# Routed attention and a spectral gate on one core: pairwise start, PV in pairs, a re-buffered last batch

## The chip, the core and the metric

The kernel runs on one core of a Trainium2 chip. The metric is the time of one execution in device microseconds; "span" is the part of it that the profile covers, from the first instruction to the last (the time reads some 1.7 us above the span). The engines are PE (matmul), DVE (vector), ACT (scalar), POOL (general) and SP (issues most transfers). The program gives each engine its own list of instructions and makes it wait for others by semaphores.

## The reference, cut to what matters

```python
# q, k, v: (4, 8, 768, 64), centroids: (8, 16, 64), float32
q_assign = argmax(einsum(q / |q|, c / |c|))        # a cluster for each query
k_assign = argmax(einsum(k / |k|, c / |c|))        # and for each key
scores = where(q_assign == k_assign, q @ k.T / 8, -1e9)
attn = softmax(scores) @ v                         # (4, 8, 768, 64)
x = attn, heads side by side                       # (4, 768, 512)
x1, x2, x3 = split(x @ w_proj)                     # w_proj: (512, 1536)
conv = irfft(rfft(x2) * rfft(filter_fft))          # along the 768 positions
out = (x1 * conv * x3) @ w_out
```

## The kernel before

Heads come in eight groups of four (two groups make a batch), each in two pairs. A head pair goes through six key tiles of 128 keys. The Python code does not fix the order of instructions: it describes operations with an estimated length, a due time and the buffers they read and write, and a list scheduler (`place`) puts them in order on each engine.

```python
NPB = 6        # P tiles (one head's exp of one key tile), 6 in turn
...
# in place(): which of the operations that could start goes next on an engine
t0 = min(c[0] for c in cand)
c = min((c for c in cand if c[0] <= t0 + wait * (c[1].kind == "urgent") + 1e-9),
        key=lambda c: (c[1].due, c[1].seq))
...
# in attention(): one key tile sk of a head pair
for hp in range(2):
    def sc(e, hp=hp, sk=sk, h=h):              # scores: two matmuls of 384 columns
        ...
    op(("PE", .34), sc, ..., kind="score")
    ex = op(("ACT", .82 + ...), ...activation(T.p[s]..., Act.Exp, scale=0.125), ...)
def pv(e, sk=sk):                              # P times V: eight matmuls 128x64 by 385
    ...
op(("PE", 1.37), pv, due, ..., kind="pv")
if sk:                                         # sums of P for the denominator, per head
    for hp in range(2):
        def acc(e, hp=hp, sk=sk):
            x = T.p[slots[hp, 0]][:, :S] if sk == 1 else T.acc[hp]
            T.nc.vector.tensor_tensor(T.acc[hp], x, T.p[slots[hp, sk]][:, :S], op=Alu.add)
        op(("DVE", .95), acc, ...)
...
# in hyena(): column tile dt of a batch; yy and od have one buffer, x3 two
op(("POOL", 1.9), lambda e, dt=dt, xb=xb: T.nc.gpsimd.tensor_tensor(
    T.y2[:, dt], T.yy[:]..., T.x3[xb][:]..., op=Alu.mult), ...)
...
# the start
for z in range(4): load_qk(0, z // 2, z % 2, z * .1)
load_v(0, 2.0); routing(0)                     # all four heads at once, then 8 mask rows
for z in range(4): load_qk(1, z // 2, z % 2, 9 + z)
tables()                                       # loads of the filter, its spectrum
```

"Masks" are rows that say which cluster a query or key belongs to; they are moved into the operands of the score matmuls by transfers of 24 KB. "Routing" makes them. `tables` makes the spectrum of the filter, `hyena` is all that follows attention in a batch.

The softmax here doesn't subtract the row's maximum and nothing guards it: scores larger than these inputs give would overflow.

## Time and profile before

| | before |
|---|---|
| time, median of 3 (range) | 468.88 us (466.34 to 470.32) |
| span of the profiled run | 467.4 us |
| first exp / first PV | 34.8 / 54.7 us |
| first PV to end of last PV | 351.8 us |
| end of last PV to end | 60.9 us |
| mode changes of PE (into and out of PV, routing and denominator products) | 236 |

The profile counts an instruction's whole duration as busy time, also where POOL or DVE holds it up: an addition of 3245 ns, shown below, is in the 121.6 us of its group (64 of 1899 ns) in full. Two groups of the page matter later; after the bar stand busy us, mean ns of one, then the engine's idle time before them and what ended it:

```profile
L503 DVE TENSOR_TENSOR acc<-acc,p 128x768 f32<-128x768 f32 x128 | 127.5, 1034 | 9.5 <-ACT p L482 9.3
L667 POOL TENSOR_TENSOR y<-yy,x 128x768 bf16<-128x768 f32 x16 | 32.3, 2020 | 108.4 <-DVE yy L663 89.0
```

The additions on DVE that follow the first of a head take 1034 ns in the mean, and POOL's products 2020 where ten of the 16 take 1799 to 1832. By start and end in the trace, 132 of all 160 additions have no work of POOL beside them, and none of these takes over 960 ns. The twelve of over 1 us lie beside POOL's other large group (L622, sums of the spectrum: eight), its products (two) or its casts (two), which will matter.

### The profile page before, as it was taken

The numbers are of one execution on the slowest core, as the hardware profiler recorded it, in microseconds if no ns is written. First come the engines' busy times: TensorE is split into PE (matmuls) and PEld (weight loads), VectorE is DVE, ScalarE is ACT, GpSimd is POOL, SyncE is SP. The second block draws the span as 40 slices with busy tenths as digits, with TensorE's granted clock in tenths as the row PEclk, the third lists the DMA queues.
The fourth block names the chain that finished last, engine by engine and source line by source line (L and its number), as shares of the span: only waits on it lengthen the run. The fifth ranks groups of instructions, "written<-read, shape, count | busy, mean of one in ns | idle before, by whom it ended". The sixth has DMA issues, their size and how long they took to land. (4 is left out here: it accounts for less than half of the span.)

```text
span 467.4 us, 6821 instructions
## 1 busy us (share of the span) xinstructions
PE 417.5 (89%) x2431; PEld 180.4 (39%) x2444; DVE 361.4 (77%) x557; ACT 274.3 (59%) x418; POOL 93.0 (20%) x94
## 2 busy tenths in 40 slices
PE   4745799999999998999999899999997999889846
PEld 3422333443434444434443344434333443334412
DVE  7885767899899898896759997978769788825550
ACT  5663276877775578477954687476654456424213
POOL 4420000000100813011005322030105312202540
PEclk9895899999999999999999999999999899979977
DMA  8999500522631234115610232123110010111003
GB/s 195 231 202 238 115 14 1 138 70 53 155 84 49 72 70 102 32 36 179 183 35 19 67 70 67 41 81 127 45 37 17 1 35 3 35 79 57 1 0 135
DMA packets 67226, 37.06 MB, mean 79 GB/s; under 512 B 56636, under 2 KB 62328, under 8 KB 67192
## 3 DMA queue, kind: packets, MB, share of 16 engines
q1 hardware_dynamic: 65992, 34.50, 28.5%
q0 software_dynamic: 1056, 2.10, 2.5%
q8 instruction: 19, 0.31, 0.3%
q14 instruction: 15, 0.12, 0.1%
q10 hardware_dynamic: 144, 0.03, 0.0%
HBM read 30.66 MB, written 6.48 MB: 79 GB/s over the span
## 5 line engine op out<-in xcount | busy, mean ns | idle before, releaser
L482 ACT ACTIVATE p<-pair 128x768 f32<-128x768 f32 x192 | 149.2, 811 | 58.8 <-PE pair L478 39.9
L493 PE MATMUL pair<-p,vraw 128*64 128x385 f32 x768 | 147.6, 507 | 1.0 <-DVE hm L350 0.4
L503 DVE TENSOR_TENSOR acc<-acc,p 128x768 f32<-128x768 f32 x128 | 127.5, 1034 | 9.5 <-ACT p L482 9.3
L478 PE MATMUL pair<-aug,aug 128*128 128x384 bf16 (+1 forms) x384 | 86.3, 331 | 9.8 <-ACT p L482 4.8
L493 PEld LDWEIGHTS pair<-p,vraw 128*64 128x64 f32 x768 | 48.1, 139 | 66.6 <-issue 61.8
L622 POOL TENSOR_TENSOR y<-tm 128x512 bf16<-128x512 f32 x24 | 38.3, 1604 | 114.6 <-DVE tm L618 90.7
L478 PEld LDWEIGHTS <-aug 128*128 128x128 bf16 (+1 forms) x384 | 33.6, 98 | 54.6 <-issue 39.8
L667 POOL TENSOR_TENSOR y<-yy,x 128x768 bf16<-128x768 f32 x16 | 32.3, 2020 | 108.4 <-DVE yy L663 89.0
L634 PE MATMUL bank<-xT,wpj 128*128 128x384 bf16 x256 | 48.7, 327 | 2.8 <-DVE x L641 1.3
L387 PE MATMUL bank<-ident,qkraw 128*128 128x128 f32 x192 | 34.3, 305 | 11.9 <-DMA qkraw<-in_q_dram 10.7
L503 DVE TENSOR_TENSOR acc<-p,p 128x768 f32<-128x768 f32 x32 | 29.6, 955 | 19.3 <-ACT p L482 9.1
L220 POOL CAST aug<-qkT 64x768 bf16<-64x768 f32 x11 | 11.2, 1018 | 138.9 <-ACT qkT L218 69.7
L387 PEld LDWEIGHTS bank<-ident,qkraw 128*128 128x128 f32 x192 | 24.1, 154 | 29.5 <-issue 11.9
L618 DVE TENSOR_TENSOR tm<-bank,hm 128x512 f32<-128x512 f32 x48 | 30.5, 680 | 6.0 <-PE bank L365 4.7
L634 PEld LDWEIGHTS <-wpj 128*128 128x128 bf16 x256 | 23.6, 97 | 27.7 <-issue 13.8
L679 PE MATMUL bank<-wout,y 128*128 128x512 bf16 x91 | 26.8, 436 | 7.2 <-POOL y L667 6.0
L218 ACT COPY qkT<-bank 128x384 f32<-128x384 f32 x43 | 20.2, 479 | 16.4 <-PE bank L387 16.2
L218 ACT COPY x<-bank 128x384 f32<-128x384 f32 x23 | 11.0, 478 | 23.8 <-PE bank L634 19.3
L218 ACT CAST aug<-qkT 64x768 bf16<-64x768 f32 x28 | 23.2, 830 | 0.7
L218 ACT COPY ob<-bank 128x512 f32<-128x512 f32 x22 | 12.7, 584 | 18.0 <-PE bank L679 16.4
L605 PE MATMUL bank<-wpj,uT 128*128 128x512 bf16 x92 | 22.4, 380 | 0.7 <-DVE uv L220 0.5
L663 DVE TENSOR_TENSOR yy<-bank,od 128x384 f32<-128x384 f32 x32 | 16.3, 550 | 8.0 <-ACT od L218 5.9
(114 smaller groups left out, 397.9 us busy)
## 6 DMA issues: line engine op xcount, KB each, us to landing
qkraw<-in_q_dram SPq DMA_DIRECT2D x32, 192.0 KB
qkraw<-in_k_dram SPq DMA_DIRECT2D x32, 192.0 KB
vraw<-in_v_dram SPq DMA_DIRECT2D x8, 768.0 KB
rb<-dr SPq DMA_DIRECT2D x30, 192.0 KB
out_dram<-ob SPq DMA_DIRECT2D x11, 512.0 KB
y<-in_moe_filter_fft_dram SPq DMA_DIRECT2D x4, 384.0 KB
wpj<-in_moe_w_proj_dram POOLq DMA_DIRECT2D x1, 1536.0 KB, 12.2
aug<-ohT SPq DMA_DIRECT2D x64, 24.0 KB
```

The source lines that it names most:

```text
L218: T.nc.scalar.copy(out, in_)
L387: T.nc.tensor.transpose(ap(h)[:, ts(t, 128)], T.qkraw[s][:, 3 * ch + t].rearrange("p h d -> p (h d)"), T.ident)
L478: T.nc.tensor.matmul(two(h)[:, ch, :384], ag[1][:K, ts(sk, 128)], ag[0][:K, ts(ch, 384)], start=True, stop=True)
L482: ex = op(("ACT", .82 + (1.28 if first[0] is None else 0)), lambda e, h=h, s=s: T.nc.scalar.activation(T.p[s][:, :S].rearrange("p (a b) -> ...
L493: T.nc.tensor.matmul(o[64 * hp:64 * hp + 64, ch, :385], T.vraw[aset][:, 2 * pr + hp, sk * D:(sk + 1) * D], T.p[slots[hp, sk]][:, 384 * ch: ...
L503: T.nc.vector.tensor_tensor(T.acc[hp], x, T.p[slots[hp, sk]][:, :S], op=Alu.add)
L605: T.nc.tensor.matmul(ap(h), f[:, e_, kt, ts(m, 128)], T.wpj[:, kt, DM:2 * DM], start=(kt == 0), stop=(kt == ND - 1))
L618: op(("DVE", .68), lambda e, i=i, cs=cs, r=r, h=h: T.nc.vector.tensor_tensor(T.tm[r][:, cs], ap(h), T.hm[:, i, 2 * r + cs], op=Alu.mult), ...
L622: op(("POOL", 1.45), lambda e, i=i, r=r: T.nc.gpsimd.tensor_tensor(T.y[:, i, r], T.tm[r][:, 0], T.tm[r][:, 1], op=Alu.add), due + 2, r=[(" ...
L634: T.nc.tensor.matmul(ap(h)[:, :384], T.wpj[:, kt, off + dt * 128:off + dt * 128 + 128], T.xT[xs][:, kt, ts(ch, 384)], start=(kt == 0), sto ...
L667: op(("POOL", 1.9), lambda e, dt=dt, xb=xb: T.nc.gpsimd.tensor_tensor(T.y2[:, dt], T.yy[:].rearrange("p t c -> p (t c)"), T.x3[xb][:].rear ...
L679: T.nc.tensor.matmul(ap(h), T.y2[:, kt, ts(2 * tt + e_, 128)], T.wout[:, kt], start=(kt == 0), stop=(kt == ND - 1))
```

## The change

Its intent is in three parts. At the start, the first group is routed by pairs of heads, so that the first pair's masks need not wait for the second; loads and masks of the first group go out by two issuing engines (SP and ACT), and the loads of the filter and of the third group are held back until the masks are out. In the middle, P is kept for both heads together in four pairs, one addition of 1536 replaces two of 768, and the scheduler prefers a second PV right behind a first. At the end, the last batch's sums are split in three quarters and a quarter, its column tiles have buffers of their own, and DVE may do what POOL did. Smaller parts come along: V is loaded per head pair into three buffers, and the scheduler's estimates of PE's work are corrected.

```diff
-NPB = 6
-NQK = 5
+NPB = 4            # P pairs
+NQK = 4
...
-                c = min((c for c in cand if c[0] <= t0 + wait * (c[1].kind == "urgent") + 1e-9),
-                        key=lambda c: (c[1].due, c[1].seq))
+                c = min((c for c in cand if c[0] <= t0 + wait + 1e-9), key=lambda c: (
+                    c[1].due - (bonus if e == "PE" and st.last == "pv" == c[1].kind else 0.0)
+                    + (c[0] - t0) * 20, c[1].seq))          # bonus=4.0
...
+        return [op({"SP": .8, "ACT": .8} if n == 0 else ("SP", .8), lambda e, hp=hp: dma(e)(
...
+    def first_masks(pr):                      # routing of one pair of the first group
...
-            due = A(i0 + sk + 1) + .7
+            due = A(i0 + (sk | 1) + 1) + .7    # PV of tiles 0,1 / 2,3 / 4,5 due together
...
-                for hp in range(2):
-                    def acc(e, hp=hp, sk=sk):
-                        x = T.p[slots[hp, 0]][:, :S] if sk == 1 else T.acc[hp]
-                        T.nc.vector.tensor_tensor(T.acc[hp], x, T.p[slots[hp, sk]][:, :S], op=Alu.add)
-                    op(("DVE", .95), acc, ...
+                def acc(e, sk=sk):
+                    x = T.p[slots[0]][:, :, :S] if sk == 1 else T.acc[:]
+                    T.nc.vector.tensor_tensor(T.acc[:], x, T.p[slots[sk]][:, :, :S], op=Alu.add)
+                op(("DVE", 1.75), acc, ...
...
-            w0, w1 = A(96) + 6, A(96) + 8
+            w0, w1 = A(96) - 20, A(96) - 10    # last batch due early
+                if last and 2 * m + e_ < NU:   # U: sum over three quarters, then the last
+                    op(("PE", .647), lambda e, U=U: U(e, range(3)), ...
+                    op(("PE", .217), lambda e, U=U: U(e, range(3, 4)), ...
...
+            if last:                            # x3 of the last batch in qkT, four buffers
+                x3, xkeys = (lambda dt=dt: T.qkT[dt][:]), ...
+            if last and dt % 2:                 # yy and od a second buffer each (sim, rb)
...
+            op({"POOL": 1.9, "DVE": .95} if last else ("POOL", 1.9), ...   # y2 product
...
-    tables()
+    tables(got)                                 # got: the first group's mask operations;
+                                                # the loads concerned come after them
```

## The prediction

> **What bounds the kernel now.** I read the page's busy shares first, then the slices, then busy time in three stretches, then instructions in order of time at both ends.
>
> ```profile
> PE 417.5 (89%) x2431; PEld 180.4 (39%) x2444; DVE 361.4 (77%) x557; ACT 274.3 (59%) x418; POOL 93.0 (20%) x94
> PE   4745799999999998999999899999997999889846
> PEclk9895899999999999999999999999999899979977
> 0.00:54.70 54.70, 30.38 (x180) 17.73 (x181) 43.77 (x85) 27.15 (x47) 13.76 (x46) 0.88 0.97 201
> 54.70:406.20 351.50, 342.55 (x2027) 142.79 (x2036) 294.20 (x432) 229.62 (x341) 63.49 (x38) 0.99 0.24 65
> 406.20:467.40 61.20, 44.54 (x227) 19.86 (x227) 23.39 (x41) 17.49 (x31) 15.75 (x11) 0.86 0.13 52
> ```
>
> The columns of the last three lines are the stretch and its length, then busy us of PE, PEld, DVE, ACT and POOL, the granted clock, the DMA share and GB/s. I cut at the first PV matmul (54.7 us) and at the end of the last (406.2 us). Between the two, PE is busy for 342.6 of 351.5 us: PE is the bound there. At the two ends it is not: 54.7 us pass before the first PV, and 61.2 us after the last.
>
> How much of that is real work? The spacing of starts where nothing waits gives units: score tile (two matmuls) 0.33 us, PV of one key tile 1.35, three transposes 0.36, a routing product 0.67, a spectrum or gate product 0.65, U and W 0.86, an inverse pair 1.19, denominator 0.68. Counted by these over the order of issue, the head holds 21.6 us of PE work in 54.7, the middle 335.7 in 351.5, the tail 37.9 in 61.2. So 33, 16 and 23 us are lost in the three.
>
> Why the head is late, in order of time:
>
> ```profile
> 27.56 5.43 SPq L452 DMA_DIRECT2D aug<-ohT  x8
> 34.10 0.63 PE L478 MATMUL pair<-aug,aug 80*128 80x384 bf16 x2 [3.98 <-DMA aug<-ohT]
> 41.33 1.51 PE L387 MATMUL bank<-ident,qkraw 128*128 128x128 f32 x6 [5.14 <-DMA qkraw<-in_q_dram]
> 54.74 5.80 PE L493 MATMUL pair<-p,vraw 128*64 128x385 f32 x24 [0.41 <-DVE hm L350]
> ```
>
> The eight mask rows are issued at 27.56 and the first score runs at 34.10[...]. PE then stands behind a transpose of the third group, whose load competes with the weights, and the filter tables come before the first PV.
>
> Why the tail is long:
>
> ```profile
> 410.00 1.49 PE L516 MATMUL bank<-acc,ones 128*32 128x384 f32 x4 [2.69 <-DVE acc L503]
> 442.14 1.80 POOL L667 TENSOR_TENSOR y<-yy,x 128x768 bf16<-128x768 f32 x1 [4.38 <-DVE yy L663]
> 446.61 1.80 POOL L667 TENSOR_TENSOR y<-yy,x 128x768 bf16<-128x768 f32 x1 [2.66 <-DVE yy L663]
> 451.07 1.80 POOL L667 TENSOR_TENSOR y<-yy,x 128x768 bf16<-128x768 f32 x1 [2.66 <-DVE yy L663]
> 454.10 1.80 POOL L667 TENSOR_TENSOR y<-yy,x 128x768 bf16<-128x768 f32 x1 [1.23 <-DVE yy L663]
> 455.96 7.17 PE L679 MATMUL bank<-wout,y 128*128 128x512 bf16 x21 [2.42 <-POOL y L667]
> ```
>
> One buffer each of x3 (two), yy and od makes the four column tiles take turns, about 4.5 us each, with POOL's 1.8 us product inside; the output product waits for all four.
>
> [...]
>
> ```profile
> 61.22 1.52 PE L493 MATMUL pair<-p,vraw 128*64 128x385 f32 x8
> 62.67 0.82 PE L478 MATMUL pair<-aug,aug 80*128 80x384 bf16 x4
> 63.42 1.52 PE L493 MATMUL pair<-p,vraw 128*64 128x385 f32 x8
> 403.68 2.86 PE L493 MATMUL pair<-p,vraw 128*64 128x385 f32 x16
> 406.47 0.84 PE L516 MATMUL bank<-acc,ones 128*32 128x384 f32 x4
> ```
>
> One PV takes 1.45 us until the next kind starts, two take 2.79: the second adds 1.34, so about 0.10 is the change. Two score tiles ahead of PV take 0.75, not 0.65: 0.10 again.
>
> [...] Here a pair of q/k loads takes 1.4 to 1.8 us to issue, 0.39 MB or 222 to 285 GB/s, and the engines move 222 GB/s from 5 to 10 us; two queues can save little. [...] the trace has 955 for the first additions, and 1034 in the mean for the others. [...] 0.50 from 35 to 40 us, and the six transposes at 41.33 took 1.51 us against 0.83 at 26.42.
>
> **The change, part by part.** *PE work.* Nothing large is removed. Counted over the order of issue, PV comes in 74 runs instead of 93, of which 21 hold two or more (the rest are still single), and the mode changes fall from 236 to 203: 33 x 0.10 = 3.3 us less. Routing by pairs adds 6 + 6 short transposes, 1.1 us. Net -2.2.
>
> *Head.* In the new order PE has before its first PV only 15.9 us of work: 16 transpose triples instead of 20, no spectrum products, two score key tiles instead of four. V, filter and third-group loads no longer stand ahead: the queue holds group 0, V of one group and group 1, 3.9 MB, and the filter is held until the masks have landed. At 222 to 230 GB/s from about 2 us it is empty near 19 us (estimate). ACT now sets the time. Summing its list from the first transposed tile (5.3 us): 15 evacuations and sim copies x 0.48 = 7.2, inverse copies 1.4, four 64-row casts x 0.83 = 3.3, nine sine pieces 4.3, three table loads x 1.28 = 3.8, four mask issues x 0.6 = 2.4, small 0.3; together 22.7, so the first exp comes at 28 without waits, and I say 29.5 with some, against 34.8. Two key tiles of exp (4 x 0.86) later, PV starts at 33.5 instead of 54.7. Of these 21.2 us, 5.7 are work put off; 15.5 are gain.
>
> *Middle.* Work 335.7 + 5.7 - 2.2 = 339.2. Before, loss was 15.8, mostly DVE and ACT lateness around the spectrum products; I keep 15. DVE gets 80 additions of 1536 for 160 of 768[...]. PE is the bound, so this helps only where DVE holds P. New cost: in the order before, every PV has one key tile of scores issued ahead; in the new one the second PV of a run often has none. In the first two head pairs (12 key tiles) the pattern is four score tiles, two PVs, and again. There the four exps (4 x 0.81, after 0.65 us from score to exp) plus the last PV make about 5.5 us per two key tiles against 4.2 of PE work. Six such periods lose 1.3 each, 8 us, of which fillers (denominator, routing, spectrum) take back about 3. I charge 5. So the last PV ends at 33.5 + 339.2 + 15 + 5 = 392.7.
>
> *Tail*, from the last PV's end, PE work the same 37.9. Denominator, transpose and reciprocal to 3.1, broadcast to 5.5, with the three-quarter sums of U for two banks beside them and for two more after; scale and uT on DVE to 7.5; rest of U to 9.6; spectrum to 13.5. DVE then has 12 products x 0.66, three additions x 0.68, two gate products x 0.55, 11 us from 10.5, and some waits for POOL's 1.3 us additions: 22.5. PE fills this with 8 gate and 5 output products to 23. Then I, I, gates, I, gates, I to 33; DVE runs all four column tiles with own buffers and its own 0.95 us products, the third at 36.4 and the fourth at 38.4. Output sums over three tiles start at 36.5, the rest ends at 41.7, evacuation at 42.5, and the last store takes the 3.6 us it takes now. 46 us; with small waits 47.5 against 61.2.
>
> Sum: 392.7 + 47.5 = 440.2 of span; the runs read 1.5 above the span (468.9 against 467.4): 441.7, say 441.
>
> **Rivals.** (1) The PV pairs lose more than they save: no scores are ahead, ACT's exps end the waits, and in blocks with little filler (14 to 16 us of PE work per six key tiles) each second PV waits 0.3 to 1.3 us. About 40 such places at the upper end cost 20 us more than I charge: 455. Against it: most blocks have other work between, and ACT is only 59% busy. (2) DVE becomes the bound: in blocks with spectrum products its list sums to 30 us beside PE's 31.7, and it did so before. This would give back 5 to 8 us. (3) The head is bound by bytes: masks are quick, but loads, weights (4.2 MB) and filter still have to come, and PE waits for the third group later. Its first transpose now stands after the twelfth key tile, near 60 us; all bytes are in by 57 at 225 GB/s, so close, up to 3 us. (4) Better: the wider P ring (eight tiles for six) absorbs DVE's lateness, middle loss falls to 10, no loss in the first blocks: 431.
>
> **Range and chances.** Head and tail gains of 15.5 and 13.7 are each good to about 5, the middle to 8 in either direction; together about 10. Range 430 to 452. To be within 2% (above 459.5) two of the rivals would have to hit together. Faster 0.96, same 0.03, slower 0.01.
>
> **What would show it.** First exp between 28 and 31 us and ACT nearly gapless before; first PV between 32 and 36; no PE wait over 2 us for a q load between 30 and 60. In the first 12 key tiles, score groups waiting for exp, period above 5 us for two. A run of two PVs 2.8 us long. [...] From last PV to end 46 to 49 us, with column tiles overlapping and the last four output quarters right behind DVE's fourth product. It is wrong if the middle loses over 30 us to ACT, or if the first PV is later than 40.

Passages are cut from this text where they told of the hardware what no trace of this case shows. No term of the sum is among them: it came to 392.7 + 47.5 = 440.2 us of span, 441 of time. What the traces show in their place:

- The mask rows. The text gave loads ahead of them in the queue as the reason for their delay, and the trace does not bear it out: all 5.7 MB that SP had issued before them were on their way by 28 us, half a us after the first row's issue. From then on the weights (issued at 25.3 and 26.3 us) moved some 0.4 MB in two us and SP's queue 0.22 MB in all from 30 to 38 us, and the first score waited 3.98 us for a row. The weights' last bytes came at 41 us, which is what "competes" can rest on for the third group.
- A "change" is PE's step between PV and another kind of product. Its 0.10 us was measured for PV beside scores and denominator products alone; as the price of all 33 it is an estimate.
- That two issuing engines can save little is an estimate from the two rates beside it. 0.50 is the granted clock of PE.
- The new additions had one length, and their sum, by a formula that no trace shows. Neither was in the sum above, as PE was held to be the bound. The trace of the kernel before has two DVE operations on 1536 columns of float32 that take 1753 ns (`L339`), which could have served.
- Of DVE's times at the end, 0.95 and 0.68 us are estimates from its additions of 768 columns (955 ns) and its products of 512 (680). Measured later: 951 to 959 ns for the four products, 902 in the mean for the three additions.

## The result, and the profile after

The changed kernel takes 451.06 us in the median of 4 runs (449.07 to 453.68), against 469.6 in the median of 4 for the kernel before beside it. The ratio is 0.962 (95% interval 0.955 to 0.969). A ratio is the mean time of one kernel's fast runs over that of the other's of the same rounds, so it is not quite the ratio of the medians. So it is faster by 3.8%: inside the predicted range of 430 to 452, but at its upper end, 10 us above the 441 that I named.

Busy time in the three stretches of the changed kernel, cut at its own first PV and the end of its last (columns as in the prediction), after the page's busy shares and slices:

```profile
PE 413.2 (91%) x2443; PEld 182.0 (40%) x2456; DVE 360.3 (80%) x485; ACT 270.4 (60%) x413; POOL 96.9 (21%) x93
...
PE   4788888998999999999999999986999999989975
```

```profile
0.00:35.60 35.60, 24.50 (x143) 15.22 (x143) 24.87 (x57) 22.74 (x41) 17.75 (x49) 0.86 0.72 145
35.60:402.40 366.80, 348.53 (x2078) 148.30 (x2086) 304.81 (x381) 231.07 (x343) 73.39 (x41) 1.00 0.31 78
402.40:451.90 49.50, 40.16 (x225) 18.52 (x227) 30.59 (x49) 16.62 (x30) 5.76 (x4) 0.95 0.17 65
```

From its own first PV to the end of its own last (402.5 us; 406.5 before, 0.3 after the prediction's cut), the start is 19.1 us shorter, the end 11.5, the middle 15.1 us longer. Some of the last is work put off: 5.7 us by the prediction's count. DVE is as busy as before, although it has 72 instructions fewer. In PE's slices there is one hollow in the middle (8 and 6 in the 27th and 28th slices, 294 to 316 us), which the kernel before does not have.

The start in order of time: the first pair's masks go out at 24.19, the second pair's from ACT at 28.89, and the first exp follows at 33.00, the first PV at 35.6.

```profile
25.00 2.68 PE L462 MATMUL bank<-ident,qkraw 128*128 128x128 f32 x12
28.89 1.41 ACTq L391 DMA_DIRECT2D aug<-ohT  x2
30.92 1.44 PE L549 MATMUL pair<-aug,aug 80*128 80x384 bf16 x4 [2.01 <-ACT qkT L220]
33.00 1.51 ACT L553 ACTIVATE p<-pair 128x768 f32<-128x768 f32 x2
```

The first score waits 2.01 us for ACT, which makes a score operand only after it has issued two mask rows (1.41 us). PE runs at half clock here (granted 0.50 from 20.6 to 27.4 us): twelve transposes take 2.68 us, and 1.53 in a run below whose clock is whole at this point.

The first key tiles, where PVs come in pairs, and the larger of the two groups of additions (the other has 16 of 1816 ns):

```profile
41.96 2.81 PE L564 MATMUL pair<-p,vraw 128*64 128x385 f32 x16
...
46.10 0.48 PE L549 MATMUL pair<-aug,aug 80*128 80x384 bf16 x2 [0.57 <-ACT p L553]
...
47.22 2.81 PE L564 MATMUL pair<-p,vraw 128*64 128x385 f32 x16
```

```profile
L575 DVE TENSOR_TENSOR acc<-acc,p 128x1536 f32<-128x1536 f32 x64 | 121.6, 1899 | 11.3 <-ACT p L553 9.6
```

Two PVs in a run take 2.81 us, the scores between wait for exps, and the period is 5.26 us (the next one 5.54), as predicted. The additions take 1883 ns in the mean of all 80, but 1750 in that of the 52 that have no work of POOL beside them.

The end: DVE's first product (y2) comes 33.7 us after the last PV, behind the last gate products in its list, which wait for PE (1.93 us the longest). The fourth starts at 441.11, and PE's last output products, of which this is the last group, follow one by one. The first fence is DVE, the second PE.

```profile
436.25 0.96 DVE L757 TENSOR_TENSOR y<-yy,qkT 128x768 bf16<-128x768 f32 x1 [0.77 <-PE bank L769]
```

```profile
440.13 6.61 PE L769 MATMUL bank<-wout,y 128*128 128x512 bf16 x22 [1.61 <-DVE y L757]
```

The hollow: in each stretch of six key tiles I took the length less the work that PE did in it by the prediction's units. Some matmul records are missing (92 of 96 output products have one in the control), so these losses are good to about half a us. The loss is mostly 0 to 3 us and at most 5.1 in both kernels, but for two stretches of the changed one. The second loses 5.6 us (4.2 when the work is counted over the order of issue, in which no record is missing); a loss was expected there. And a stretch of 38.6 us around 300 us holds 30.2 of work and loses 8.4. The kernel before loses 0.8 in its stretch of the same heads (24.8 us).

```profile
296.79 2.06 POOL L757 TENSOR_TENSOR y<-yy,x 128x768 bf16<-128x768 f32 x1 [12.41 <-DVE yy L753]
297.10 1.97 DVE L504 TENSOR_TENSOR oh<-oh,revc 128x384 bf16<-128x384 bf16 x1
...
307.44 5.03 DVE L575 TENSOR_TENSOR acc<-acc,p 128x1536 f32<-128x1536 f32 x2
307.61 3.25 POOL L757 TENSOR_TENSOR y<-yy,x 128x768 bf16<-128x768 f32 x1 [8.76 <-DVE yy L753]
...
312.99 0.85 PE L588 MATMUL bank<-acc,ones 128*32 128x384 f32 x8 [1.93 <-DVE qkT L222]
```

The first pair is a y2 product of the second batch on POOL and a step of routing that takes 0.29 to 0.35 us elsewhere and 1.97 here. The second pair is two additions and the next product. By itself each of the two additions reads:

```profile
L575 DVE TENSOR_TENSOR acc<-acc,p x2: 1749/2497/3245, 307.4 to 309.2; 128x1536 f32<-128x1536 f32 x2
```

(shortest, median and longest in ns, then when the first and last start). The first takes its usual 1749 and POOL, started 0.17 us later, is held until it ends at 309.2; POOL then needs 1.67 us, until 310.86; the second addition starts at 309.2 and ends at 312.45, one usual length after POOL. So in this place the two take turns, to 0.2 us: the one that started first takes its usual time and the other ends one usual length after it. The first pair fits: POOL's product ends at 298.85 us, and the step of routing, started 0.31 us after it, at 299.07. What makes them take turns the traces do not show. The scheduler provides for it: it keeps operations marked `lock` (these additions, this routing step, POOL's products) apart, and in its plan none of DVE's 190 runs beside one of POOL's 52. They meet because the execution departs from the plan. PE waits for the masks (1.16 us, at 306.50), for exps, and for DVE (1.93 us, the last line above).

### The profile page after: what moved, and what is told of

Its sections match the earlier page's. It is cut to its first block, busy times and chain, and to the rows that moved or that the text cites. A ratio compares the mean times of both kernels' runs of the same rounds, so it can differ in the third digit from the quotient of the medians.

```text
span 451.9 us, 6707 instructions
## 1 busy us (share of the span) xinstructions
PE 413.2 (91%) x2443; PEld 182.0 (40%) x2456; DVE 360.3 (80%) x485; ACT 270.4 (60%) x413; POOL 96.9 (21%) x93
## 3 DMA queue, kind: packets, MB, share of 16 engines
q1 hardware_dynamic: 62856, 33.62, 28.7%
## 4 chain that ended last, share of the span: by engine, by line
PE 67%; DVE 19%; ACT 6%; issue 5%; DMA 1%; ACTq 0%; DVEq 0%
PE pair L564 22%; PE pair L549 10%; PE bank L722 8%; DVE acc L575 6%; PE bank L769 5%; PE bank L677 4%; PE bank L462 4%; PE bank L747 4%; ACT p L553 3%; PE bank L588 2%; PE bank L482 2%; PE bank L376 2%; DVE tm L695 2%; DVE osb L637 2%; DVE uT L648 1%
## 5 line engine op out<-in xcount | busy, mean ns | idle before, releaser
L564 PE MATMUL pair<-p,vraw 128*64 128x385 f32 x768 | 140.9, 497 | 0.4 <-ACT osb L580 0.4
L575 DVE TENSOR_TENSOR acc<-acc,p 128x1536 f32<-128x1536 f32 x64 | 121.6, 1899 | 11.3 <-ACT p L553 9.6
L699 POOL TENSOR_TENSOR y<-tm 128x512 bf16<-128x512 f32 x21 | 34.7, 1662 | 106.9 <-DVE tm L695 106.3
L549 PEld LDWEIGHTS <-aug 128*128 128x128 bf16 (+1 forms) x384 | 33.0, 98 | 59.3 <-issue 45.3
L222 POOL CAST aug<-qkT 64x768 bf16<-64x768 f32 x19 | 23.7, 1246 | 119.2 <-ACT qkT L220 101.6
L757 POOL TENSOR_TENSOR y<-yy,x 128x768 bf16<-128x768 f32 x12 | 27.8, 2321 | 97.4 <-DVE yy L753 82.8
L220 ACT COPY qkT<-bank 128x384 f32<-128x384 f32 x53 | 24.9, 481 | 22.7 <-PE bank L462 9.8
L575 DVE TENSOR_TENSOR acc<-p,p 128x1536 f32<-128x1536 f32 x16 | 29.1, 1816 | 9.3 <-ACT p L553 4.7
L462 PEld LDWEIGHTS bank<-ident,qkraw 128*128 128x128 f32 x192 | 25.3, 158 | 17.7 <-POOL aug L817 5.3
L695 DVE TENSOR_TENSOR tm<-bank,hm 128x512 f32<-128x512 f32 x48 | 30.2, 683 | 2.6 <-PE bank L380 1.3
L769 PE MATMUL bank<-wout,y 128*128 128x512 bf16 x92 | 25.1, 417 | 2.9 <-DVE y L757 2.5
L747 PE MATMUL bank<-inv,y 128*128 128x384 bf16 (+1 forms) x128 | 19.9, 327 | 1.5 <-ACT x L220 0.6
L580 ACT COPY osb<-pair 128x770 f32<-128x770 f32 x16 | 12.8, 802 | 12.4 <-PE pair L564 12.4
L753 DVE TENSOR_TENSOR yy<-bank,od 128x384 f32<-128x384 f32 x28 | 14.3, 548 | 6.8 <-ACT od L220 6.3
```

What stands on the lines that cost most here:

```text
L220: T.nc.scalar.copy(out, in_)
L462: T.nc.tensor.transpose(ap(h)[:, ts(t, 128)], T.qkraw[s][:, 3 * ch + t].rearrange("p h d -> p (h d)"), T.ident)
L549: T.nc.tensor.matmul(two(h)[:, ch, :384], ag[1][:K, ts(sk, 128)], ag[0][:K, ts(ch, 384)], start=True, stop=True)
L564: T.nc.tensor.matmul(o[64 * hp:64 * hp + 64, ch, :385], T.vraw[vs][:, hp, sk * D:(sk + 1) * D], T.p[slots[sk]][:, hp, 384 * ch:384 * ch + ...
L575: T.nc.vector.tensor_tensor(T.acc[:], x, T.p[slots[sk]][:, :, :S], op=Alu.add)
L695: op(("DVE", .68), lambda e, i=i, cs=cs, r=r, h=h: T.nc.vector.tensor_tensor(T.tm[r][:, cs], ap(h), T.hm[:, i, 2 * r + cs], op=Alu.mult), ...
```

## The experiments

All of the twelve kernels were correct. The times are medians of the fast runs with the ratio to the kernel before of the same rounds; below, "control" is the changed kernel. The twelve ran in three rounds on three chips, and the control was repeated in one of them only; elsewhere a difference of 2 or 3 us from it rests on the ratios. Where two profiles are compared, PE's clock must be looked at as well: it differs between them. In the traces of the two kernels it is halved in stretches of 3.4, 6.8 and 10.2 us.

### The pairs of PVs: less and more preference

Edit: `bonus=4.0` to `bonus=0.0`, and to `bonus=8.0`. By the order of instructions, PV then comes in 82 and 67 runs (control 74, kernel before 93), with 217 and 187 mode changes (203), and 5 and 25 PVs have no score tile issued ahead (17).

> The changed kernel with the preference for a second PV set to zero; all else as changed. In the order of issue the PVs then come in 82 runs for 74, mode changes are 217 for 203 (1.4 us more of PE work), and only 5 PVs for 17 start with no scores ahead; in the first 12 key tiles one for six. Theory A (the second PV of a run waits for ACT, and this made the middle 27.5 us lossy): first to last PV falls from 366.8 to about 360, the whole to about 445. Rival B (the loss is DVE and POOL slowing each other, the pairs are as good as they were meant): 452 to 453, slower by the 1.4 us of changes.

> The opposite dose: preference 8 for 4. 67 PV runs, 187 mode changes (1.6 us less), 25 PVs without scores ahead for 17. Theory A: eight more such waits of 0.5 to 1.2 us cost more than is saved, 453 to 457. Rival B: 449 to 450.

Measured: without preference 451.75 us (ratio 0.967, 0.964 to 0.970; its profiled run is not used), with double preference **440.64** us (0.9435, 0.940 to 0.947). Rival B has the first (452 to 453) and both theories miss the second. What follows: PVs without scores ahead do not cost what a rival of my prediction feared, as the kernel with most of them is the fastest. But nor is it the number of mode changes: from 203 to 187 they are worth 16 x 0.10 = 1.6 us of the 11. The trace shows where the rest is. Its first PV is at 33.5 us, 360.6 us pass until the end of the last, 45.3 after it. Against the control's profile the start is 2.1 us shorter, the middle 6.3 and the end 4.1; about 6.4 of these 12.5 us are a clock that was halved in the control's profile (all of the start, where the order is the control's, and 2.6 and 1.7 us of the rest, see below), 6.1 the order. The stretch that lost 8.4 us loses 2.7. At the end, DVE's list has its first product between gate products, at 421.15 us, and the last at 430.00, where the control has them all behind (DVE, then PE):

```profile
421.15 0.96 DVE L757 TENSOR_TENSOR y<-yy,qkT 128x768 bf16<-128x768 f32 x1
```

```profile
428.24 5.35 PE L769 MATMUL bank<-wout,y 128*128 128x512 bf16 x24
```

The output products run without a wait (5.35 us for 24), where the control takes from 437.27 to 446.74 for them. So of the part that is order, 1.6 us are mode changes by the prediction's price, and the other 4.5 lie in which work the scheduler happened to put next to which. Whether an order with fewer waits also keeps the clock up, no run shows; all five runs of this kernel had a clock of 0.991 or more.

### The end as before

Edit: the conditions on the last batch made false and its due times restored, so no split sums, no own buffers, products and additions on POOL (`if last:` to `if False:`, `{"POOL": 1.9, "DVE": .95} if last else ("POOL", 1.9)` to `("POOL", 1.9)`, `A(96) - 20` to `A(96) + 6`, and so on); the order of PV and scores is kept.

> The changed kernel with the last batch as before: shared x3, yy and od buffers, products on POOL, no split sums, old due times; head and middle keep the same order of PV and scores. Theory: the tail from the last PV returns to about 61 us from 49.5, so the whole is 462 to 464. Rival (the tail gain hangs on the middle's new order): under 457.

Measured: 455.69 us (0.975, 0.971 to 0.979); 53.3 us after the last PV, against 49.4 of the control and 60.9 of the kernel before. The end's own changes are worth 3.9 us in the trace (and some 4 in time), not 11, and this is rather too much: both profiles have PE's clock halved at their last products, but this one by more (7.05 us for 21 of them, the control 6.61 for 22; 4.71 and 4.92 in runs below whose clock is whole there), which is some 0.6 us. The other 7.6 us of the shorter end come with the rest of the change. Of these, 5.0 have arisen by the spectrum of x2, which starts 20.0 us after the last PV in the kernel before and 15.1 here. Two causes can be read off: in the kernel before, the second half of the denominator waits 2.69 us for additions and starts 3.5 us after the first (shown in the prediction), and here all of it starts 0.3 us after the last PV: DVE is not behind. And before, the clock is halved right after that (0.53 from 410 to 417 us), where here it is whole (1.00 from 400 to 438 us).

```profile
398.99 0.85 PE L588 MATMUL bank<-acc,ones 128*32 128x384 f32 x8 [0.30 <-DVE acc L575]
...
440.89 7.05 PE L769 MATMUL bank<-wout,y 128*128 128x512 bf16 x21 [2.64 <-POOL y L757]
```

The two waits for POOL at the output products (3.24 us, and 2.64 in the line above) are like those of the kernel before (3.58 and 2.42 us there).

### The first group routed jointly

```diff
-            if n == 0 and u == 4:
-                got = first_masks(0)
...
-        if n == 0:
-            return got + first_masks(1)
-        b0 = end - 20
+        b0 = end - 20 if n else 10.5
```

> The changed kernel with the first group routed jointly as before, still two load queues and the filter held until the masks landed. Theory (pair routing gets the masks out earlier): first exp 3 to 6 us later than 33.0, whole 455 to 458. Rival (ACT's list sets the first exp, and pairs only add two 64-row copies): first exp within 1.5 us of 33.0 and whole within 2 us of 451.

Measured: 454.83 us (0.973, 0.970 to 0.976); first scores 29.3, first exp 30.4, first PV 35.9 us. Joint routing makes the first exp no later. PE's clock is halved here too (0.84 granted from 20 to 31 us, 0.66 from 31 to 36), so its first PV is to be held against the control's 35.6. Against the control's 451 to 452 us, measured on other chips and with intervals that overlap, this is some 3 us in time at most, and not by the way that the prediction counted on. Nor is it the pairs alone: the scheduler makes another order of everything, on PE from the fourth operation on (197 mode changes for 203).

### The control again, and POOL's products of the middle batch on DVE

The control unaltered, on another chip; and the same order of every engine, but with the four y2 products of the second of the four batches (the "middle batch" of the texts), two of which fall in the hollow, made by DVE in the same places:

```diff
+    for o in order:
+        if o.kind == "mul1":
+            o.on = "DVE"
```

> The changed kernel again, unaltered, as the control for the three runs beside it on this chip. Expected: 451 us, ratio to before 0.962, between 0.955 and 0.969. Theory C (the stall near 300 us is tied to POOL's long products of the middle batch beside VectorE) expects its block of key tiles at that place to be some 38 us long again, against 24.8 us in the kernel before; if the stall is chance, it is gone or elsewhere in this run.

> The order of every engine's operations is the changed kernel's, but the four products of the middle batch that POOL makes near 300 us are made by VectorE at the same places of the order. Theory C (POOL's products stretch VectorE's operations, the group routing and the additions, and PE waits for masks and for the buffers of the exponentials) expects the loss of that block to fall from 8.4 us to 5 or less and the time by 3 to 5 us against the control. Rival (the block is long because the exponentials have no score tiles ahead of them there, whatever POOL does) expects within 1 us of the control.

Measured: control 452.09 us (0.968, 0.962 to 0.974), with the stretch in question 38.6 us long again. With the products on DVE: 448.65 us (0.960, 0.954 to 0.966), and that stretch is 35.4 us long: loss 5.2, down by 3.2. Theory C holds in its direction. PE still waits for masks (1.16 us, at 302.39) and for DVE (the first line), but the two additions are back to 3.54 us (the second):

```profile
308.24 0.85 PE L588 MATMUL bank<-acc,ones 128*32 128x384 f32 x8 [1.31 <-DVE qkT L222]
```

```profile
303.31 3.54 DVE L575 TENSOR_TENSOR acc<-acc,p 128x1536 f32<-128x1536 f32 x2
```

But not all of the 3.2 us is POOL and DVE taking turns. Two runs below (filter early, no split) have POOL's products in place, the same order in this stretch, and lose 6.5 us there. The difference from 8.4 is PE's clock: it is halved for 3.4 us in the middle of the waits. In the control that falls on long output products (315:320 us: granted 0.75; a group of them takes 3.3 us from 314.73, and 1.89 with the filter early); there it falls where PE waits anyway (305:310 us: granted 0.72, PE busy for 3.72 of 5 us). The control, then the run with the filter early, over the same eight us of each one's program:

```profile
312.00:320.00 8.00, 6.79 (x30) 2.51 (x32) 5.94 (x7) 5.27 (x8) 0.00 (x0) 0.79 0.09 31
```

```profile
309.00:317.00 8.00, 6.55 (x37) 2.62 (x38) 6.40 (x7) 6.17 (x10) 0.00 (x0) 1.00 0.19 69
```

So of the hollow's 8.4 us, about 1.3 to 1.5 are the taking turns (36.9 to 35.4 us), 1.7 to 1.9 the clock, and 5.2 remain, in which PE waits for masks and exps and has no score tiles ahead, whoever makes the products. I did not separate these further.

### No hold on the loads

```diff
-    got = routing(0)
+    routing(0)
+    got = ()
```

> The loads of the filters and of the third group are not held back until the first routing is made. If holding them back is what brought the first scores forward (theory H), the first scores come 3 to 6 us later than in the control and the time rises by 2 to 5 us. Rival: the head is bound by the chain routing, masks, scores and not by bytes; first scores within 1 us, time within 1.5 us.

Measured: 461.33 us (0.988, 0.982 to 0.994). First scores at 50.1 us, first PV at 54.8, where the kernel before has it. This is far beyond theory H: the hold is the part on which the whole gain of the start hangs. Of the 19 us, 12 come back in the middle (354.6 us instead of 366.9), because filter products and transposes have been made by then; 6.5 us remain between the two profiles and 9.2 between the medians.

```profile
49.42 0.88 PE L462 MATMUL bank<-ident,qkraw 128*128 128x128 f32 x3 [7.62 <-DMA qkraw<-in_q_dram]
50.09 1.49 PE L549 MATMUL pair<-aug,aug 80*128 80x384 bf16 x4
...
54.81 3.67 PE L564 MATMUL pair<-p,vraw 128*64 128x385 f32 x13
```

PE stands 7.62 us before a transpose of the third group, whose load has not landed, and the first scores stand behind it in its list.

### The last batch's products on POOL again

Edit: `{"POOL": 1.9, "DVE": .95} if last` back to `("POOL", 1.9)`, and likewise the additions.

> The last batch's gate products go back from VectorE to POOL, the split sums and own buffers stay. If moving them to VectorE is what shortened the end (theory T), the part after the last PV grows from 49.4 us to 54 or more and the time by 4 to 7 us against the control. Rival, seen in the changed kernel's trace, where VectorE's in-order list holds the products back behind others (PE waits 1.6 us at the last output products): the end grows by at most 2 us.

Measured: 453.0 us (0.971, 0.965 to 0.976); 50.8 us after the last PV, 1.4 more than the control. Of this, 1.0 is put down to the clock: the last 22 output products take 7.61 us where the control's take 6.61 (4.92 at a whole clock), with no other wait between them.

```profile
441.89 7.61 PE L769 MATMUL bank<-wout,y 128*128 128x512 bf16 x22 [1.38 <-POOL y L757]
```

The rival holds: moving them to DVE is worth little, some 0.4 us, because DVE's list puts them late.

### All loads and masks from one issuing engine

```diff
+    for o in order:
+        if o.kind in ("load", "mask"):
+            o.on = "SP"
```

> Order of every engine as in the changed kernel, but all loads and mask rows of the first group are issued by SP alone, none by ACT. The prediction held that the second queue can save little: expected first exp within 1 us of the changed kernel's 33.0 and a time within 1 us of it (ratio to before 0.962 to 0.970). Rival (the second queue is what brings the first scores forward): first exp 2 to 4 us later and the time too.

Measured: 449.14 us (0.957, 0.952 to 0.962). First scores at 28.5, first exp at 30.0 us: earlier than with two, not later. The rival falls. The reason is in ACT's list:

```profile
27.82 0.83 ACT L220 CAST aug<-qkT 64x768 bf16<-64x768 f32 x1
...
29.96 1.51 ACT L553 ACTIVATE p<-pair 128x768 f32<-128x768 f32 x2
```

Here the last cast before the exps follows ACT's copies at once, at 27.82; in the control it comes at 30.85, with 1.41 us of issuing masks before it. First scores no longer wait for ACT (0.20 us, for DVE). How much earlier depends on the clock. In the two runs above that have the control's start and a whole clock from 16 us on (the end as before, products on DVE) the first exp comes at 30.8 and 31.0 us; in the control, halved from 21 to 27 us (0.68 granted from 20 to 31), at 33.0; this run is halved for as long, about 20 to 26 us (0.70). So the gain is 0.8 us at least and 3.0 against the profile whose clock is most like it. First PV, at 32.9, is no earlier than the 32.8 and 33.0 of those two, and the time gains no more than its interval.

### The filter's loads ahead of the masks

Only SP's list changes: the four filter loads stand before the first mask row.

```diff
+    flt = [o for o in order if o.kind == "filter"]
+    order = [o for o in order if o.kind != "filter"]
+    i = next(i for i, o in enumerate(order) if o.kind == "mask")
+    order[i:i] = flt
```

> The four filter loads (1.6 MB) are issued before the mask rows, as in the kernel before, and nothing else moves on any engine. If the hold in the changed kernel works by keeping bytes out of the way (theory bytes), first scores come 3 us or more later. If it works only by the order of work that it makes the engines take (theory order: in the run without the hold, PE's list had the filter products and a transpose of the third group, which waited 7.6 us for its load, ahead of the first scores), first scores move by less than 1 us and the time by less than 1 us.

Measured: 449.26 us (0.961, 0.956 to 0.966), first scores at 29.9 us. With the control's start and its hold they come at 28.7 and 28.9 us in the two runs with a whole clock, at 29.85 in the run without the split (below), whose clock is like this one's, and at 30.9 in the control. So the filter's bytes cost 1.2 us at most and 0.1 between like clocks, and the hold works by the order of work that the scheduler makes from it. The prediction had both, bytes and order; theory bytes falls for the filter. For the loads of the third group and of the second group's V, which the hold also covers, it was not tried alone.

This run has the control's order on PE, ACT, DVE and POOL, and shows what the clock did to the control's start:

```profile
24.79 1.53 PE L462 MATMUL bank<-ident,qkraw 128*128 128x128 f32 x12
...
33.98 2.49 PE L564 MATMUL pair<-p,vraw 128*64 128x385 f32 x14
```

The same twelve transposes take 1.53 us instead of 2.68, and the first PV comes at 34.0 instead of 35.6. But this start is not at a whole clock either. Three transposes a little before, here and then in the run with products on DVE:

```profile
21.79 0.85 PE L462 MATMUL bank<-ident,qkraw 128*128 128x128 f32 x3
```

```profile
21.04 0.50 PE L462 MATMUL bank<-ident,qkraw 128*128 128x128 f32 x3
```

The views print 1.00 for all of this start. But the clock's record does not begin with the trace (in the control's it begins at 17.2 us), and the views print 1.00 for all before it. With a whole clock, in the second of these runs, the first PV comes at 33.0.

### No split sums at the end

Edit: `if last and 2 * m + e_ < NU:` and the `if last:` of the output products to `if False:`.

> The last batch's U and output products are not split into a three-quarter sum and a last quarter; own buffers and VectorE's products stay. If the split earns its part of the tail, the time from the last PV to the end grows from 49.4 us by 2 to 4 us. Rival, from the changed kernel's trace (the last output products still wait one after the other for the gate products of VectorE): by less than 1.5 us.

Measured: 450.0 us (0.9615, 0.957 to 0.966); 48.3 us after the last PV. The runs with the split and a whole clock there have 47.7 (DVE's products, one queue, filter early). This one's clock was halved for 3.4 us soon after the last PV (0.66 from 403 to 408 us). So the split is worth 0.6 us at most, as the rival said, unless it is its absence that let the clock fall, which is not shown. The last output products wait for DVE either way.

```profile
437.87 4.71 PE L769 MATMUL bank<-wout,y 128*128 128x512 bf16 x21 [1.96 <-DVE y L757]
```

### Both improvements together

Edit: `bonus=8.0`, and the second batch's four products on DVE as above.

> The preference for a second PV doubled (as in the run with 8, which took 440.6 us) and the middle batch's four products on VectorE. If the stretch of VectorE's operations beside POOL still costs time in that order, 437 to 440 us; if the new order has already stepped out of its way, as its loss of 2.7 us in the block near 300 us suggests, 440 to 442.

Measured: 442.43 us (0.945, 0.941 to 0.950), 440.6 of span against 439.4. No gain over the double preference alone: that order loses 2.7 us in the stretch near 300 us with POOL's products and without. The version with `bonus=8.0` alone, 440.64 us, beats both kernels.

## Why the prediction was right or wrong

The direction, the range and the mechanisms at start and end held. The sum missed by some 10 us. The table sets its terms beside the control's profile and beside one with the same order on PE and a clock that was halved for less of the time (filter early; all in us). A profiled run reads 1.8 us above its own span, not the 1.5 that I took.

| term | predicted | control | same order, less halved |
|---|---|---|---|
| first PV | 33.5 | 35.6 | 34.0 |
| first PV to end of last | 359.2 | 366.9 | 364.3 |
| after the last PV | 47.5 | 49.4 | 47.7 |
| span | 440.2 | 451.9 | 446.0 |

- **The clock, 5.9 of 11.7 us.** 1.6 at the start, 2.6 in the middle, 1.7 at the end (the last 22 output products 6.61 us instead of 4.92, with no other wait before them). The other runs of the control spread from 448.0 to 453.6 us with granted clocks of 0.99 down to 0.98, so this is not a fixed cost of the change. And the control's profile is of the slowest of its four runs (453.68 us): their median, 451.06, is 3.3 us above the profiled run with the filter early (447.77). The control's profile loses time to the clock in all three places (granted 0.86 before the first PV, 0.75 from 315 to 320 us, 0.95 after the last PV). The control again has 0.89 over its first 31 us and 0.72 from 315 to 320, the one with products on POOL 0.73 there. The one with the filter early loses none in the middle (0.72 from 305 to 310, in PE's waits) and at the end (1.00 from 436 to 443), and at the start 1.0 to 1.2 us (first PV 32.8 and 33.0 where the clock is whole). What decides when the clock is halved no run here shows. My prediction had the halved clock of the kernel before (0.50 from 35 to 40 us) and then put nothing for it in its sum.
- **The middle's loss, 5.1 us: the step that failed.** Predicted 15 + 5 on work of 339.2, measured 364.3 - 339.2 = 25.1. The 5 for the first twelve key tiles was near: those stretches lose 2.5 and 5.5 us (2.4 and 4.2 counted over the order of issue), against 1.6 and 0.0 before, so 5.0 to 6.4 more. What the 15 did not hold is one stretch near 300 us, which loses 6.5 instead of 0.8; all others together are 0.6 to 2 us better than I had them. Shown: 1.3 to 1.5 of it is DVE and POOL taking turns. Not settled: the rest. My guess that loss stays what it was, when every operation's place is chosen anew, was the weak point; the same scheduler with another preference gives 2.7 there.
- **The additions.** I took one undisturbed length for the new ones and the measured, disturbed busy time for the old. They take 1883 ns in the mean, so they save 6.4 us of DVE (157.1 to 150.7). In the control's trace 52 of the 80 have no work of POOL beside them; these take 1750 ns in the mean and 1761 at most. At that length all 80 would take 140.0 us and save 17.1, so the excess, 10.7 us in all, lies in the 28 that have some. What of it reaches PE is measured for two places alone: the 1.3 to 1.5 us above.
- **Start.** First PV right to 0.5 us (34.0; 0.5 to 0.7 early at a whole clock), but by two errors that cancel, so this is luck. The first exp comes 1.3 to 1.5 us late at a whole clock (30.8 and 31.0 for 29.5), 2.5 with the filter early (32.0). And I put 4.0 us between first exp and first PV, for two key tiles of exps; the runs show 2.0 (32.01 to 33.98), with the exps of one key tile between. I counted ACT's issues of masks as list time but not that they stand between the last copies and the cast that scores need; one queue brings the first exp to 30.0. The hold gives the gain, by order; routing by pairs and the second queue give the start nothing that the runs show.
- **End.** 47.5 predicted, 47.7 at a whole clock. But the sum came right for partly wrong reasons. I ascribed the gain to own buffers, split sums and DVE's products; together they give some 3.3 us with the clock's share taken out, of which the split 0.6 at most and DVE's products some 0.4; the own buffers were not run alone. The rest came from DVE being up to date at the last PV, and by the traces partly from the clock (0.86 in the end before, 0.95 after).
- **PV in runs and the rivals.** Durations as predicted (2.81 us for two). The rival that feared PVs without scores ahead falls. "DVE becomes the bound" is half true: not by its sum, but where it waits for POOL. "Head bound by bytes" falls for the filter. The wider P ring did not remove loss; three pairs, or five, were not run.

What stays open: why the run without preference takes as long as the control (its only trace is slow), and what 5 us of waiting in the stretch near 300 us would need.

## What to carry to other kernels

In a kernel whose order comes from a list scheduler, predict the order's local accidents as a term of its own, of one to two per cent here, and try several settings of a preference before reading a gain into one: here one constant moved the time by 11 us, more than the end's whole rework with its 3.9. Holding loads back mattered here through the instruction that waits for one of them in PE's list (7.62 us), and not through the filter's bytes, so look first at what stands before the critical instruction on its engine. Profile a program several times before explaining 2 us, and compare where the clock was halved; where the clock's own record starts late, the duration of a known instruction tells it.
